# Re-planning the prologue of a two-branch mixer kernel: load order, late memsets, interleaved transposes, and w3 work between the last kv tiles

## The chip, the cores and the metric

One core of one Trainium2 chip. The metric is the device time of one execution in microseconds. "Span" is the time that the profile covers, about 2 us less than the device time. Engines: PE (TensorE), ACT (ScalarE), DVE (VectorE), POOL (GpSimd), SP (its queue issues most DMAs).

## The reference, cut to what matters

```python
x = A_x; xn = layernorm(x)                       # 2048 x 448
# branch A, linear attention, 16 heads of 28
q, k, v = split(xn @ wqkv)
phi(t) = concat(softmax(t @ w_phi), softmax(-(t @ w_phi)))
kv = phi(k)^T v ; z = sum(phi(k))
A = (phi(q) kv / (phi(q) z + 1e-6)) @ wo
# branch B
h  = gelu(layernorm(xn) @ w1); hs = shift(h) @ w2; x1 = xn + hs
B  = x1 + gelu(layernorm(x1) @ w3) @ w4
out = x + A + B
```

## The kernel before

A recorder notes each operation with the 32-byte granules of each half of the partitions that it reads and writes, keeps program order on each engine, and puts semaphore waits where granules overlap. So where a memset stands in the program decides what waits for it. All elementwise operations show as one helper line (L198), activations as L194, matmuls as L186, transposes on PE as L190, plain DMAs as L204.

The parts that the change touches (cuts marked `# ...`):

```python
GRAIN = 32
# ... hT is 4 chunks of S+8 columns, bf16; gelu writes hT[:, m, 2 + 512*g : ...]
R.dma(wphi ..., "ACT")
load_x(0, 2); load_x(2, 2)
load_rows(wqk, A_wqkv[:, 0:896])             # q and k weights, rows of 1792 bytes
load_rows(w1, B_w1)
load_x(4, 4); load_x(8, 4)
load_rows(wv, A_wqkv[:, 896:1344]); load_x(12, 4)
# ... on POOL, ahead of everything else:
R.ew(pool, "memset", xn[:, :, D:512], 0.0)
# ... masks
R.ew(pool, "memset", hT[:, :, 0:2], 0.0)
R.ew(pool, "memset", hT[:, :, S + 2:S + 4], 0.0)
# ... g_tok, vaug, kvq pads

ln1_stats(0, 2); ln1_stats(2, 2); ln1_apply(0, 2, [dve]); ln1_apply(2, 2, [dve])
for t in (1, 0):
    for pair in range(2):
        weight_T(t, pair)                    # transposes wq, wk: 8 on PE, 1 copy on ACT
phi_blocks()
for i in range(4):
    xn_T(i)                                  # 4 transposes on PE into bank 0 or 1, 1 copy on ACT
ln1_stats(4, 4); ln1_stats(8, 4); ln1_apply(4, 4, [pool, dve])
for g in range(NG):
    for m in range(NM):
        w1_chunk(g, m)                       # 4 matmuls, gelu on ACT
        if g < 2:
            fold(1 - g, m)                   # 4 small matmuls, copy on ACT
    # ... stats and apply of later tiles
    for i in range(4 * g + 4, min(4 * g + 8, NT)):
        xn_T(i)
    if g < 2:
        for i in range(4 * g, 4 * g + 4):
            v_tile(i)
for i in range(NT + 2):                      # the k phase
    if i < NT:
        k_tile(i)
    if i >= 2:
        kv_tile(i - 2)
    # ... v_tile or w2_tile, q_chunk
kv_copy()
rot[0] = (3, 4, 7)                           # accumulation banks of w2 and final tiles
# ... four groups of 14 w3 chunks, with num, w2 and final tiles between them;
# num_tile uses banks 5 and 6
```

A tile is 128 tokens, a chunk 112 or 128 columns of a weight for the 512 tokens of a group; there are four groups. `xn_T` transposes a tile of xn, and its copy out of PSUM is xnT. `fold` multiplies a part of wk or wq with w_phi, so `k_tile` and `q_chunk` give phi(k) and phi(q) at once. `kv_tile` adds one tile's phi(k)^T v, `kv_copy` and `kv_blocks` bring the sum into the form (kvq) that `num_tile` needs for the numerator and denominator of A, and the final tiles are the last two products and the sum. A bank is one of the kernel's eight PSUM buffers.

The softmax here doesn't subtract the row's maximum and nothing guards it: scores larger than these inputs give would overflow.

## Time and profile before

| | before |
|---|---|
| device time | 219.07 us median of 4 runs (218.12 to 219.85) |
| the profiled run | 217.17 us, span 215.1 us |
| PE busy | 194.1 us, 90% of the span |
| k phase starts | 46.58 us |
| first num tile starts | 98.55 us |

The page's busy line of PE, then PE's busy tenths and the granted clock in 40 slices of 5.4 us:

```profile
PE 194.1 (90%) x1161; PEld 108.2 (50%) x1161; DVE 115.5 (54%) x259; ACT 94.9 (44%) x168; POOL 93.2 (43%) x125
...
PE   0469798798999998959999999999999999999994
...
PEclk9997999999999999999999999999999999999999
```

PE is the bottleneck, its idle time is mostly in the first ten slices and at the 18th, and the clock dips once, in the fourth slice. The page prints full clock until the trace's first clock record, which is at 12.24 us in this trace. PE was at half clock before it: the 32 transposes that start at 8.37 us take 3.96 us, 0.12 us each, and the eight that start at 12.58 take 0.62, 0.08 each.

The timeline (start, duration, engine, line, operation, output and inputs, count; in brackets the idle time just before and what ended it; names are those of buffers, some of them shared: `hi<-in_A_wqkv` is wqk, `w` stands for w1, w2 or w3):

```profile
3.85 0.26 POOL L198 MEMSET hT<- 128x8 bf16 x2
...
8.37 3.96 PE L190 MATMUL bank<-ident,hi 128*112 128x128 bf16 x32 [8.37 <-DMA hi<-in_A_wqkv_dram]
...
15.72 1.28 ACT L194 ACT_TABLE_LOAD   x1
...
17.75 0.60 ACT L194 ACTIVATE hT<-bank 112x512 bf16<-112x512 f32 x1 [0.74 <-PE bank L186]
...
27.07 1.03 PE L186 MATMUL bank<-xnT,w 128*112 128x512 bf16 x4
...
32.98 0.80 PE L190 MATMUL bank<-ident,xn 128*128 128x128 bf16 x8 [1.05 <-ACT xnT L194]
...
41.53 0.80 PE L190 MATMUL bank<-ident,xn 128*128 128x128 bf16 x8 [0.82 <-ACT xnT L194]
43.08 3.66 PE L186 MATMUL bank<-xnT,w 128*112 128x512 bf16 x16 [0.76 <-ACT xnT L194]
46.58 0.92 PE L186 MATMUL bank<-wpk,xnT 128*128 128x448 bf16 x4
...
94.59 0.56 PE L186 MATMUL bank<-phik,vaug 128*128 128x224 bf16 x4 [2.18 <-POOL phik L198]
...
98.55 0.62 PE L186 MATMUL bank<-kvq,eq_lo 112*128 112x128 bf16 x8 [0.36 <-DVE kvq L198]
```

To be seen: hT's pads are cleared at 3.85 us and nobody ever waits for them; the second group's first w1 chunk starts at 27.07; three waits for xnT copies (two banks, four tiles in a row) stand between 32 and 43 us; the k phase starts at 46.58; the last kv tile waits 2.2 us for POOL.

The stretches (start:end, length, busy time and count of PE, PEld, DVE, ACT and POOL, granted clock, DMA share, GB/s), the first of which is where the clock dips:

```profile
15.60:19.00 3.40, 3.24 (x11) 1.87 (x12) 3.23 (x10) 2.42 (x4) 1.42 (x3) 0.51 1.04 340
...
92.00:98.50 6.50, 4.00 (x29) 2.11 (x26) 4.30 (x8) 3.84 (x6) 5.40 (x8) 1.00 0.02 5
```

### The profile page before, as it was taken

Reading aid. Unit: us, or ns where it says so; the run is one execution under the profiler, and the core shown is the slowest. Engines: PE = TensorE matmul, PEld = TensorE weight load, DVE = VectorE, ACT = ScalarE, POOL = GpSimd, SP = SyncE. Lnnn points to the kernel's source line nnn. Section 1 sums busy time; section 2 is a strip of 40 time slices with the busy share of each in tenths; the row PEclk is TensorE's granted clock in tenths of the full one; section 3 lists DMA queues with packets and bytes.
Section 4 is the critical chain, followed back from the end, with each engine's and each line's share of the span. In section 5 each row is a group of like instructions: output and inputs, shape, how many; then the busy total and the mean of one; then the engine's idle time right before and its main releaser. Section 6 shows DMA issues by size and latency. Waiting matters only on the chain.

```text
span 215.1 us, 3027 instructions
## 1 busy us (share of the span) xinstructions
PE 194.1 (90%) x1161; PEld 108.2 (50%) x1161; DVE 115.5 (54%) x259; ACT 94.9 (44%) x168; POOL 93.2 (43%) x125
## 2 busy tenths in 40 slices
PE   0469798798999998959999999999999999999994
PEld 0345465454666555635555545545555555555552
DVE  6479624007788886867995654733552435414121
ACT  2197574869566666754443312332342234222000
POOL 7806800004566897575228333039213331235310
PEclk9997999999999999999999999999999999999999
DMA  5999900000000013002231312302531111102101
GB/s 180 318 301 301 285 13 0 0 5 0 0 0 3 0 35 63 0 3 49 57 68 24 70 47 52 70 21 49 72 71 44 33 42 46 46 21 52 43 21 43
DMA packets 26987, 13.70 MB, mean 64 GB/s; under 512 B 18398, under 2 KB 26526, under 8 KB 26974
## 3 DMA queue, kind: packets, MB, share of 16 engines
q1 hardware_dynamic: 26512, 13.49, 24.9%
q8 instruction: 9, 0.15, 0.3%
q10 hardware_dynamic: 462, 0.03, 0.2%
q14 instruction: 4, 0.03, 0.0%
HBM read 7.48 MB, written 1.84 MB: 43 GB/s over the span
## 4 chain that ended last, share of the span: by engine, by line
PE 77%; DVE 7%; ACT 5%; POOL 5%; DMA 3%; issue 1%; SPq 0%
PE bank L186 74%; POOL phik L198 3%; DMA hi<-in_A_wqkv_dram 3%; DVE st L198 3%; PE bank L190 3%; DVE ksum L198 2%; POOL g_tok L198 1%; ACT phik L194 1%; DVE mv L198 1%; ACT hi L194 1%; ACT xnT L194 1%; ACT hT L194 1%; ACT L194 1%; DVE kvq L198 1%; DVE rks L198 1%
## 5 line engine op out<-in xcount | busy, mean ns | idle before, releaser
L194 ACT ACTIVATE phik<-bank 128x512 bf16<-128x512 f32 (+1 forms) x88 | 49.2, 581 | 68.0 <-PE bank L186 68.0
L198 DVE TENSOR_TENSOR vaug<-bank,vaug 128x464 f32<-128x464 f32 (+2 forms) x64 | 33.3, 520 | 43.0 <-PE bank L186 27.6
L186 PE MATMUL bank<-gT,w 128*128 128x512 bf16 x224 | 53.9, 379 | 0.0
L186 PE MATMUL bank<-w,phik 128*128 128x448 bf16 x224 | 45.0, 352 | 0.0
L198 POOL TENSOR_TENSOR phik<-phik,rks 128x896 bf16<-128x896 bf16 x16 | 27.1, 1698 | 35.8 <-DVE rks L198 35.6
L198 POOL TENSOR_TENSOR xnT<-vaug 128x448 bf16<-128x448 f32 x16 | 15.1, 942 | 59.1 <-DVE vaug L198 59.1
L186 PEld LDWEIGHTS bank<-w,phik 128*128 128x128 bf16 x224 | 21.9, 98 | 20.9
L186 PEld LDWEIGHTS bank<-gT,w 128*128 128x128 bf16 x224 | 21.2, 98 | 21.6
L198 DVE TENSOR_REDUCE ksum<-phik 128x32 f32<-128x896 bf16 x16 | 17.3, 1083 | 19.0 <-ACT phik L194 19.0
L194 ACT ACTIVATE hi<-bank 112x512 bf16<-112x512 f32 (+1 forms) x20 | 12.4, 681 | 14.4 <-PE bank L186 7.4
L198 POOL TENSOR_TENSOR vaug<-xn,xtok 128x448 f32<-128x448 bf16 x16 | 16.5, 1031 | 5.3 <-DVE vaug L198 5.3
L186 PE MATMUL bank<-xnT,w 128*112 128x512 bf16 x64 | 17.0, 407 | 1.4 <-ACT xnT L194 1.4
L186 PE MATMUL bank<-xnT,wpq 128*112 128x512 bf16 x64 | 16.4, 379 | 0.0
L186 PE MATMUL bank<-w,hT 112*128 112x448 bf16 x64 | 14.8, 353 | 0.0
L186 PE MATMUL bank<-wo,xnT 128*128 128x448 bf16 x64 | 14.7, 352 | 0.0
L186 PE MATMUL bank<-wpk,xnT 128*128 128x448 bf16 x64 | 14.7, 352 | 0.0
L194 ACT ACTIVATE hT<-bank 112x512 bf16<-112x512 f32 x16 | 9.6, 598 | 10.9 <-PE bank L186 10.8
L198 DVE CAST vaug<-bank 128x448 bf16<-128x448 f32 x16 | 9.5, 593 | 8.6 <-PE bank L186 7.8
L186 PE MATMUL bank<-wv,xnT 128*128 128x448 bf16 x64 | 13.7, 352 | 0.0
L186 PE MATMUL bank<-phik,vaug 128*128 128x224 bf16 x64 | 8.8, 259 | 3.7 <-POOL phik L198 3.7
L198 DVE RECIPROCAL vaug<-bank 128x16 f32<-128x16 f32 x16 | 4.0, 250 | 14.2 <-PE bank L186 14.2
L190 PE MATMUL bank<-ident,hi 128*112 128x128 bf16 x32 | 3.8, 312 | 8.5 <-DMA hi<-in_A_wqkv_dram 8.4
(63 smaller groups left out, 204.6 us busy)
## 6 DMA issues: line engine op xcount, KB each, us to landing
out_dram<-vaug SPq DMA_DIRECT2D x16, 112.0 KB, 1.7
w<-in_B_w_dram SPq DMA_DIRECT2D x1, 1568.0 KB, 15.1
xtok<-in_A_x_dram SPq DMA_DIRECT2D x3, 448.0 KB, 7.4
w<-in_B_w_dram SPq DMA_DIRECT2D x1, 1344.0 KB, 11.7
hi<-in_A_wqkv_dram SPq DMA_DIRECT2D x1, 672.0 KB, 6.4
xtok<-in_A_x_dram SPq DMA_DIRECT2D x2, 224.0 KB, 3.1
w<-in_B_w_dram SPq DMA_DIRECT2D x1, 392.0 KB, 8.5
w<-in_B_w_dram SPq DMA_DIRECT2D x1, 336.0 KB, 6.9
```

The lines of the kernel that those rows point to most:

```text
L186: self.op("PE", lambda e: e.matmul(out, lhsT, rhs, start=start, stop=stop, skip_group_check=True), [out], [lhsT, rhs])
L190: self.op("PE", lambda e: e.transpose(out, in_, ident), [out], [in_, ident])
L194: self.op("ACT", lambda e: e.activation(out, in_, func, **kw), [out], [in_] + aps)
L198: self.op(eng, lambda e: getattr(e, name)(out, *args, **kw), [out], aps)
```

## The change

The intent: let PE start earlier (wk first and alone, on a second queue; only its 16 transposes ahead of the first group; memsets that are not needed yet moved behind the norms), keep it from waiting for xnT copies (transposes put between v tiles and w1 chunks), and cover the waits at the end of the k phase with w3 chunks.

```diff
-        R.dma(wphi ..., "ACT")
-        load_x(0, 2)
+        load_x(0, 2)
+        R.dma(wphi ..., "ACT")
+        load_c(wqk[:, :, D:2 * D], A_wqkv[:, D:2 * D], "ACT")
         load_x(2, 2)
-        load_rows(wqk, A_wqkv[:, 0:896])
         load_rows(w1, B_w1)
+        load_rows(wqk[:, :, 0:D], A_wqkv[:, 0:D])
         load_x(4, 4)
+        load_rows(wv, A_wqkv[:, 896:1344])
         load_x(8, 4)
-        load_rows(wv, A_wqkv[:, 896:1344])
# ... POOL: only ident, mhalf, xn[:, 0:4] pads, rsel and masks stay in front; the rest becomes
+        def late_1(): ...   # xn[:, 4:NT] pads
+        def late_2(): ...   # half of vaug's pads, then both hT pads
+        def late_3(): ...   # the other half of vaug, g_tok, kvq
-        for t in (1, 0):
-            for pair in range(2):
-                weight_T(t, pair)
         phi_blocks()
+        weight_T(1, 0); weight_T(1, 1)
         for i in range(4):
             xn_T(i)
+        late_1()
         ln1_stats(4, 4)
+        ln1_apply(4, 4, [pool, dve])
+        late_2()
+        for m in range(NM):
+            w1_chunk(0, m); fold(1, m)
+            if m % 2 == 1:
+                weight_T(0, m // 2)
+        ln1_stats(8, 4)
+        v_tile(0); xn_T(4); xn_T(5); v_tile(1); xn_T(6); v_tile(2); xn_T(7); v_tile(3)
# ... groups 1 to 3 in the same manner; for group 2: w1, two xn_T, w1, two xn_T, w1, w1
# the k phase: the last two kv tiles and kv_copy leave the loop
-        rot[0] = (3, 4, 7)
+        rot[0] = (3, 4)                      # num_tile takes its two banks from 5, 7, 6
+            if g == 0: steps = [             # one entry after each w3 chunk
+                    [kv_tile(14)], [kv_tile(15), kv_copy], [], [kv_blocks],
+                    [g_apply(4..7)], [num_tile(0)], [w2_tile(8), g_T(4), g_T(5)], [num_tile(1)],
+                    [w2_tile(9), g_T(6), g_T(7), o_T(0)], [num_tile(2)], [w2_tile(10), o_T(1)],
+                    [num_tile(3)], [w2_tile(11), ln_scale(8..11)], [o_T(2)]]
```

No matmul is added or removed. The built program shows one thing that the diff does not say: ACT's load of the gelu table now waits for POOL.

```
ACT, before:  5 L194 LoadActFuncSet
              6 L194 Activation hT<-bank 112x512 [waits s_PE]
ACT, after:   7 L194 LoadActFuncSet [waits s_POOL]
              8 L194 Activation hT<-bank 112x512 [waits s_PE]
```

More of the change, by code (lines that the diff above doesn't have):

```diff
@@ L330, in load_rows, with load_c @@
             R.dma(dst[0:64, 3, :], src[384:448, :])
+        def load_c(dst, src, eng):
+            R.dma(dst[:, 0:3, :], src[0:384, :].rearrange("(c p) d -> p c d", p=128), eng)
+            R.dma(dst[0:64, 3, :], src[384:448, :], eng)
+        load_x(0, 2)
         R.dma(wphi[0:DH, :].rearrange("e (h f) -> e h f", h=H), A_w_phi.rearrange("h e f -> e h f"), "ACT")
-        load_x(0, 2)
+        load_c(wqk[:, :, D:2 * D], A_wqkv[:, D:2 * D], "ACT")
         load_x(2, 2)
-        load_rows(wqk, A_wqkv[:, 0:896])
         load_rows(w1, B_w1)
+        load_rows(wqk[:, :, 0:D], A_wqkv[:, 0:D])
         load_x(4, 4)
+        load_rows(wv, A_wqkv[:, 896:1344])
         load_x(8, 4)
-        load_rows(wv, A_wqkv[:, 896:1344])
         load_x(12, 4)
@@ L344, in bass_parallel_sum__linear_kernel_hedgehog__mixer_s_mlp__prompt_kernel @@
         R.dma(w4[:, :, :], B_w4.rearrange("(c p) d -> p c d", p=128))
+        mb = maskb[0:CR, :].rearrange("p (h e) -> p h e", h=4)
+        rv = rsel[0:DH, :].rearrange("p (h e) -> p h e", h=4)
+        vp = vaug.rearrange("p t (h e) -> p (t h) e", e=HP)
+        kq = kvq[0:CR, :, :].rearrange("p b (h e) -> p b h e", e=HP)
         R.ew(dve, "memset", wqk[64:128, 3, :], 0.0)
@@ L354, in bass_parallel_sum__linear_kernel_hedgehog__mixer_s_mlp__prompt_kernel @@
              [ident], [ident])
-        R.ew(pool, "memset", xn[:, :, D:512], 0.0)
         R.ew(pool, "memset", mhalf[:, :], -0.5)
+        R.ew(pool, "memset", xn[:, 0:4, D:512], 0.0)
+        R.ew(pool, "memset", rsel[0:DH, :], 0.0)
+        R.op(pool, lambda e: e.affine_select(rv, rv, pattern=[[0, 4], [-1, DH]], compare_op=ALU.not_equal,
+                                             fill=1.0, base=0, channel_multiplier=1), [rsel[0:DH, :]], [rsel[0:DH, :]])
         R.ew(pool, "memset", maskb[0:CR, :], 1.0)
-        mb = maskb[0:CR, :].rearrange("p (h e) -> p h e", h=4)
         R.op(pool, lambda e: e.affine_select(mb, mb, pattern=[[-DH, 4], [0, DH]], compare_op=ALU.is_ge,
@@ L363, in bass_parallel_sum__linear_kernel_hedgehog__mixer_s_mlp__prompt_kernel, with late_1, late_2, late_3 @@
              [maskb[0:CR, :]], [maskb[0:CR, :]])
-        R.ew(pool, "memset", rsel[0:DH, :], 0.0)
-        rv = rsel[0:DH, :].rearrange("p (h e) -> p h e", h=4)
-        R.op(pool, lambda e: e.affine_select(rv, rv, pattern=[[0, 4], [-1, DH]], compare_op=ALU.not_equal,
-                                             fill=1.0, base=0, channel_multiplier=1), [rsel[0:DH, :]], [rsel[0:DH, :]])
-        R.ew(pool, "memset", hT[:, :, 0:2], 0.0)
-        R.ew(pool, "memset", hT[:, :, S + 2:S + 4], 0.0)
-        R.ew(pool, "memset", g_tok[:, :, D:512], 0.0)
-        vp = vaug.rearrange("p t (h e) -> p (t h) e", e=HP)
-        R.ew(pool, "memset", vp[:, :, DH:HP], 0.0)
-        R.ew(pool, "memset", vp[:, :, DH:DH + 1], 1.0)
-        R.ew(pool, "memset", kvq[0:CR, :, :], 0.0)
-        kq = kvq[0:CR, :, :].rearrange("p b (h e) -> p b h e", e=HP)
-        for b in range(8):
-            R.ew(pool, "tensor_copy", kq[:, b, :, DH + 1:DH + 2], mb[:, :, 0:1])
+        def late_1():
+            R.ew(pool, "memset", xn[:, 4:NT, D:512], 0.0)
+        def late_2():
+            R.ew(pool, "memset", vp[:, 0:8 * H, DH:HP], 0.0)
+            R.ew(pool, "memset", vp[:, 0:8 * H, DH:DH + 1], 1.0)
+            R.ew(pool, "memset", hT[:, :, 0:2], 0.0)
+            R.ew(pool, "memset", hT[:, :, S + 2:S + 4], 0.0)
+        def late_3():
+            R.ew(pool, "memset", vp[:, 8 * H:NT * H, DH:HP], 0.0)
+            R.ew(pool, "memset", vp[:, 8 * H:NT * H, DH:DH + 1], 1.0)
+            R.ew(pool, "memset", g_tok[:, :, D:512], 0.0)
+            R.ew(pool, "memset", kvq[0:CR, :, :], 0.0)
+            for b in range(8):
+                R.ew(pool, "tensor_copy", kq[:, b, :, DH + 1:DH + 2], mb[:, :, 0:1])
         def ln_stats(stt, mvt, src, i):
@@ L508, in num_tile @@
             r = i % 2
-            bs = [banks[5], banks[6]]
+            bs = [bank(5, 7, 6), bank(5, 7, 6)]
             for s in range(2):
@@ L557, in bass_parallel_sum__linear_kernel_hedgehog__mixer_s_mlp__prompt_kernel @@
         ln1_apply(2, 2, [dve])
-        for t in (1, 0):
-            for pair in range(2):
-                weight_T(t, pair)
         phi_blocks()
+        weight_T(1, 0)
+        weight_T(1, 1)
+        rot[0] = (5, 6, 7)
         for i in range(4):
             xn_T(i)
+        late_1()
         ln1_stats(4, 4)
-        ln1_stats(8, 4)
-        ln1_apply(4, 4, [pool, dve])
-        rot[0] = (5, 6, 7)
-        for g in range(NG):
-            for m in range(NM):
-                w1_chunk(g, m)
-                if g < 2:
-                    fold(1 - g, m)
-            if g == 0:
-                ln1_stats(12, 4)
-                ln1_apply(8, 4, [pool, dve])
-            if g == 1:
-                ln1_apply(12, 4, [pool, dve])
-            for i in range(4 * g + 4, min(4 * g + 8, NT)):
-                xn_T(i)
-            if g < 2:
-                for i in range(4 * g, 4 * g + 4):
-                    v_tile(i)
+        ln1_apply(4, 4, [pool, dve])
@@ new lines, in bass_parallel_sum__linear_kernel_hedgehog__mixer_s_mlp__prompt_kernel @@
+        late_2()
+        for m in range(NM):
+            w1_chunk(0, m)
+            fold(1, m)
+            if m % 2 == 1:
+                weight_T(0, m // 2)
+        ln1_stats(8, 4)
+        v_tile(0)
+        xn_T(4)
+        xn_T(5)
+        v_tile(1)
+        xn_T(6)
+        v_tile(2)
+        xn_T(7)
+        v_tile(3)
+        ln1_apply(8, 4, [pool, dve])
+        for m in range(NM):
+            w1_chunk(1, m)
+            fold(0, m)
+        ln1_stats(12, 4)
+        v_tile(4)
+        xn_T(8)
@@ L583, in bass_parallel_sum__linear_kernel_hedgehog__mixer_s_mlp__prompt_kernel @@
+        xn_T(9)
+        v_tile(5)
+        xn_T(10)
+        v_tile(6)
+        xn_T(11)
+        v_tile(7)
+        ln1_apply(12, 4, [pool, dve])
+        late_3()
+        w1_chunk(2, 0)
+        xn_T(12)
+        xn_T(13)
+        w1_chunk(2, 1)
+        xn_T(14)
+        xn_T(15)
+        w1_chunk(2, 2)
+        w1_chunk(2, 3)
+        for m in range(NM):
+            w1_chunk(3, m)
         rot[0] = (0, 1, 2, 3, 4, 5)
-        for i in range(NT + 2):
-            if i < NT:
-                k_tile(i)
+        for i in range(NT):
+            k_tile(i)
@@ L587, in bass_parallel_sum__linear_kernel_hedgehog__mixer_s_mlp__prompt_kernel @@
             if i >= 2:
                 kv_tile(i - 2)
-            if i < NT:
-                if i % 2 == 0:
-                    v_tile(8 + i // 2)
-                else:
-                    w2_tile(i // 2)
-                    if i % 8 == 7:
-                        ln_scale(mv2, rs2, i // 2 - 3, 4)
-                q_chunk(*divmod(i, 4))
-                if i == 9:
-                    for j in range(4):
-                        g_apply(j)
-                if i >= 12:
-                    g_T(i - 12)
@@ L602, in bass_parallel_sum__linear_kernel_hedgehog__mixer_s_mlp__prompt_kernel @@
-        kv_copy()
+            if i % 2 == 0:
+                v_tile(8 + i // 2)
+            else:
+                w2_tile(i // 2)
+                if i % 8 == 7:
+                    ln_scale(mv2, rs2, i // 2 - 3, 4)
+            q_chunk(*divmod(i, 4))
+            if i == 9:
+                for j in range(4):
+                    g_apply(j)
+            if i >= 12:
+                g_T(i - 12)
         R.ew(pool, "memset", o_tok[:, :, D:512], 0.0)
-        rot[0] = (3, 4, 7)
+        rot[0] = (3, 4)
@@ L608, in bass_parallel_sum__linear_kernel_hedgehog__mixer_s_mlp__prompt_kernel @@
                 fill.append(lambda g=g: [g_apply(4 * g + 4 + j) for j in range(4)])
-            if g == 0:
-                fill.append(kv_blocks)
             for j in range(4):
@@ L618, in bass_parallel_sum__linear_kernel_hedgehog__mixer_s_mlp__prompt_kernel @@
                 if g < 2:
-                    fill.append(lambda i=i + 8: w2_tile(i))
+                    if True:
+                        fill.append(lambda i=i + 8: w2_tile(i))
                     if j == 3:
                         fill.append(lambda i=4 * g + 8: ln_scale(mv2, rs2, i, 4))
-                if g + 1 < NG:
-                    fill.append(lambda i=i + 4: g_T(i))
+                if g + 1 < NG and j in (1, 2):
+                    fill.append(lambda i=4 * g + 2 * j + 2: [g_T(i), g_T(i + 1)])
                 if i > 0:
                     fill.append(lambda i=i - 1: o_T(i))
-            n = 0
+            if g == 0:
+                steps = [
+                    [lambda: kv_tile(14)], [lambda: kv_tile(15), kv_copy], [], [kv_blocks],
+                    [lambda: [g_apply(4 + j) for j in range(4)]], [lambda: num_tile(0)],
+                    [lambda: w2_tile(8), lambda: g_T(4), lambda: g_T(5)], [lambda: num_tile(1)], [lambda: w2_tile(9), lambda: g_T(6), lambda: g_T(7), lambda: o_T(0)],
+                    [lambda: num_tile(2)], [lambda: w2_tile(10), lambda: o_T(1)],
+                    [lambda: num_tile(3)], [lambda: w2_tile(11), lambda: ln_scale(mv2, rs2, 8, 4)],
+                    [lambda: o_T(2)]]
+            else:
+                steps = [fill[len(fill) * k // FC:len(fill) * (k + 1) // FC] for k in range(FC)]
             for fc in range(FC):
                 w3_chunk(g, fc)
-                while n < len(fill) * (fc + 1) // FC:
-                    fill[n]()
-                    n += 1
+                for f in steps[fc]:
+                    f()
         o_T(NT - 1)
```

## The prediction

> **What bounds it.** TensorE: the page gives PE 194.1 us of a 215.1 us span; the chain of waits is 77% PE, and one unbroken run of matmuls from 98.5 to 212.3 us. Only PE's idle time can be won: 21.0 us. By the timeline and the stretches: 8.4 us before the first transpose (waits for the q/k weights' DMA), 3.4 us more up to 24 us, 2.6 us in three waits between 31 and 44 us (xnT copies), 3.0 us inside the k phase (phik chain, not touched), 2.2 us at 92.4 (last kv tile waits for POOL's phik), 0.4 us at 98.2 (kvq), and the tail (not touched). Work is only reordered, nothing is removed.
>
> **End of the k phase.** Now w3 chunks (0.87 us each) stand between kv tiles 14 and 15 and before the kv blocks. phik of tile 15 is ready about 2.6 us after the last q chunk, covered by two w3 chunks and a kv tile (2.1 us): 2.2 shrinks to about 0.6, and 0.4 vanishes. Gain 1.9 us. I take back 0.3: in the first w3 group num tiles now come every two w3 chunks, about 2.9 us of PE for 3.6 us of DVE (2.2 for the num tile, 1.4 for w2 and its statistics).
>
> **Prologue.** wk alone (392 KB, second queue) should land near 6.5 instead of 8.2. By the Trainium skill ("DMA: Bandwidth & Descriptors", Issuing engines are not separate DMA queues) both queues share the same DMA engines; the trace's 300 GB/s is the limit already, so the second queue gains only order. Sixteen transposes instead of 32 precede the first xnT; the POOL norm scales no longer wait for memsets (8.58 before, about 5.7 after). The first w1 matmul moves from 15.8 to about 12.3.
>
> But most of this is given back by one dependency. The pad columns of hT are now cleared in "late_2", behind the second group's norms on POOL, and the first gelu writes the same 32-byte granule. The built order shows ACT's gelu table load waiting for POOL there. Path: x tiles 4-7 land 11.2 (same bytes ahead of them), statistics 2.9 (DVE), scale 1.5, two applies 1.4, vaug memsets about 1.1, hT: about 18.4. Then table load 1.28, so the first gelu is at about 19.7, against 17.75 before. PE fills its three w1 banks and stops about 17 to 20.8. By the skill ("TensorE: Matmul & The Clock Gate", Part 1) an idle window re-throttles the clock; in the trace before it was 0.66 between 15 and 20 us, so a slow stretch near 20 us is likely again. From there ACT limits (0.60 + 0.54 per w1/fold pair, 0.94 per weight transpose copy). Walking the banks by hand: second group's w1 at about 28.9 (27.1 before), but interleaved v tiles remove the xnT waits, and k starts near 45.9 instead of 46.6. Gain 0.7 us.
>
> **Sum.** 0.7 + 1.9 - 0.3 = 2.3 us: 216.6 us, 1.1% faster; range 213.9 to 218.5. Chances: faster by over 2% 0.17, within 2% 0.80, slower 0.03.
>
> **What would show it.** First PE work at 6 to 7 us; ACT's second table load preceded by a wait of several us for POOL, ending at 18 to 19; a PE gap of 3 to 4 us before 21; k phase starting 45 to 46.6; the wait before the last kv tile under 1 us; no gaps over 0.5 us after 100 us; PE busy about equal.
>
> **What would make it wrong.** x tiles 4-7 landing earlier or POOL quicker (a first gelu at 16 would give 3 us more); the clock staying low after the stall (up to 2 us lost); wk's DMA delaying x; two accumulation banks (3, 4) instead of three stalling w2 or the final tiles; DVE falling behind in the first w3 group.

## The result, and the profile after

The changed kernel took 213.18 us, median of 4 runs (213.00 to 213.39). The ratio to before is 0.973, 95% interval 0.969 to 0.977. A ratio here is the mean time of one kernel's fast runs over that of the other's of the same rounds, so not quite the ratio of the medians that I quote; the runs that are over 1.5% above the fastest of the same kernel are left out of it. Predicted were 216.6 us and a range that ended at 213.9: the gain was 5.9 us, not 2.3.

The page's busy line of PE, its busy tenths and the clock:

```profile
PE 195.7 (93%) x1161; PEld 108.5 (51%) x1161; DVE 116.4 (55%) x259; ACT 94.5 (45%) x168; POOL 93.4 (44%) x128
...
PE   1687899998999989999999999999999999999994
...
PEclk9999999999999999999999999999999999999999
```

The timeline, the lines that answer to those of before:

```profile
12.15 1.95 PE L186 MATMUL bank<-xnT,w 128*112 128x512 bf16 x4 [0.69 <-ACT xnT L194]
...
17.17 0.58 POOL L198 MEMSET hT<- 128x8 bf16 x2
...
17.20 1.31 PE L186 MATMUL bank<-xnT,w 128*112 128x512 bf16 x4
...
17.67 1.28 ACT L194 ACT_TABLE_LOAD   x1 [5.58 <-POOL hT L198]
...
18.97 0.60 ACT L194 ACTIVATE hT<-bank 112x512 bf16<-112x512 f32 x1
...
19.46 0.54 ACT L194 ACTIVATE wpk<-bank 128x448 bf16<-128x448 f32 x1
19.89 0.60 ACT L194 ACTIVATE hT<-bank 112x512 bf16<-112x512 f32 x1
...
20.05 0.37 PE L186 MATMUL bank<-bd,hi 112*128 112x112 bf16 x4 [1.54 <-ACT wpk L194]
...
27.20 1.07 PE L186 MATMUL bank<-xnT,w 128*112 128x512 bf16 x4
...
43.87 0.92 PE L186 MATMUL bank<-wpk,xnT 128*128 128x448 bf16 x4
...
91.86 0.56 PE L186 MATMUL bank<-phik,vaug 128*128 128x224 bf16 x4 [0.45 <-POOL phik L198]
...
96.16 0.61 PE L186 MATMUL bank<-kvq,eq_lo 112*128 112x128 bf16 x8
...
106.01 0.40 PE L186 MATMUL bank<-kvq,eq_lo 112*128 112x128 bf16 x4 [0.44 <-DVE vaug L198]
```

The clock line is not the whole truth here either. The first clock record of this trace is at 17.77 us, and until then PE was at half clock: the w1 chunk at 12.15 us takes 1.95 us, the one at 20.26 takes 1.03.

What they show, as differences of the two spans, 215.1 and 211.2 us:

- **Prologue.** The hT memset is where I feared it, and ACT waits 5.6 us for it. The second group's first w1 chunk starts at 27.20, against 27.07 before: the earlier start is used up entirely. Yet the k phase starts at 43.87 instead of 46.58, 2.7 us earlier; this is won after 27 us, where the three waits for xnT are gone.
- **End of the k phase.** From the start of the k phase to the first num tile it is now 52.3 us instead of 52.0, but six w3 chunks of 0.87 us lie in it instead of three: 2.6 - 0.3 = 2.3 us won.
- **w3 phase.** From the first num tile to the start of the last addition it was 113.7 us (212.28 - 98.55); three chunks fewer would make 111.1; it is 112.3 (208.44 - 96.16). So 1.15 us are lost, part of it in the 0.44 us wait for DVE shown above.
- 2.7 + 2.3 - 1.15 is 3.9 us, the difference of the spans. The medians differ by 5.9. The other 2 us are not in these two traces.

### The profile page after: what moved, and what is told of

Its sections match the earlier page's. It is cut to its first block, busy times and chain, and to the rows that moved or that the text cites. A ratio compares the mean times of both kernels' runs of the same rounds, so it can differ in the third digit from the quotient of the medians.

```text
span 211.2 us, 3034 instructions
## 1 busy us (share of the span) xinstructions
PE 195.7 (93%) x1161; PEld 108.5 (51%) x1161; DVE 116.4 (55%) x259; ACT 94.5 (45%) x168; POOL 93.4 (44%) x128
## 4 chain that ended last, share of the span: by engine, by line
PE 66%; DVE 13%; POOL 10%; ACT 6%; issue 2%; DMA 2%; POOLq 0%; DVEq 0%; ACTq 0%
PE bank L186 64%; DVE vaug L198 5%; DVE st L198 3%; POOL phik L198 3%; POOL g_tok L198 3%; POOL rs L198 2%; ACT hi L194 2%; DVE xn L198 2%; DVE ksum L198 2%; DMA xtok<-in_A_x_dram 2%; PE bank L190 1%; ACT phik L194 1%; ACT hT L194 1%; DVE mv L198 1%; POOL vaug L198 1%
## 5 line engine op out<-in xcount | busy, mean ns | idle before, releaser
L186 PE MATMUL bank<-xnT,w 128*112 128x512 bf16 x64 | 17.8, 418 | 0.7 <-ACT xnT L194 0.7
L186 PE MATMUL bank<-wv,xnT 128*128 128x448 bf16 x64 | 14.7, 353 | 0.3 <-ACT wpk L194 0.3
L198 POOL TENSOR_SCALAR rs<-mv 128x4 f32<-128x4 f32 (+1 forms) x18 | 3.7, 207 | 21.8 <-DVE mv L198 20.8
L198 POOL TENSOR_SCALAR g_tok<-xn,rs 128x448 bf16<-128x448 bf16 x16 | 11.2, 715 | 0.2
L194 ACT ACTIVATE eq_lo<-bank 112x512 bf16<-112x512 f32 x16 | 8.7, 596 | 5.8 <-PE bank L186 5.8
```

The source lines that it names most:

```text
L186: self.op("PE", lambda e: e.matmul(out, lhsT, rhs, start=start, stop=stop, skip_group_check=True), [out], [lhsT, rhs])
L194: self.op("ACT", lambda e: e.activation(out, in_, func, **kw), [out], [in_] + aps)
L198: self.op(eng, lambda e: getattr(e, name)(out, *args, **kw), [out], aps)
```

## The experiments

Each ran on a chip together with runs of the kernel before, whose median was 217.2 to 219.7 us on three chips. The changed kernel itself hardly moves (213.18 and 213.20 us). "Landing" times are those of the last of the 16 completions of a load in the trace's record, and half-clock windows are from its clock record; both count from the span's start.

### e0: the kernel before, again

No edit.

> The kernel before, unchanged, to see every run's clock and span. Theory A (the trace I predicted from was of a run about 2 us faster than the usual one: the profiled run took 217.17 us, the four timed ones 218.1 to 219.9): timed runs 218 to 220 us, and a profile whose prologue differs (more TensorE time at half clock, or late DMA landings). Theory B (profiled and timed runs differ by a fixed overhead): the new profile again near 217.2, spans of the timed runs near 215. If A holds, some of the 5.9 us is a matter of the baseline and not of my sum.

Measured: 219.55 us, median of 6 (216.55 to 219.90); the profiled run took 219.65, span 217.9. Its stretches:

```profile
15.00:21.80 6.80, 6.11 (x24) 3.26 (x23) 6.49 (x21) 4.08 (x7) 4.07 (x8) 0.50 1.06 286
21.80:96.90 75.10, 67.63 (x416) 40.65 (x415) 43.89 (x80) 50.91 (x98) 36.54 (x34) 1.00 0.13 32
96.90:100.30 3.40, 3.40 (x16) 1.82 (x14) 0.67 (x3) 1.19 (x2) 3.40 (x6) 0.51 0.19 40
```

Theory A holds for this pair of traces. After the first clock record the clock was at half for 6.8 us in the prologue and for 3.4 us just after the wait for the last kv tile, 10.2 us in all; in the trace that I predicted from it was 3.4 us. The k phase began at 47.94 instead of 46.58 and the stretch from there to the first num tile took 53.45 instead of 51.97: 1.36 + 1.48 = 2.8 us, the whole difference of the two spans. Same kernel, same work, no other difference.

Whether the usual run looks like this one is less clear. The record has the mean granted clock, and one 3.4 us window takes 0.008 off it. Of the 55 runs of the kernel before none reads 1.000; 44 read 0.992 (one window), nine 0.984 and two 0.976 or 0.977, like this profiled run. So a window somewhere is the rule, and three are rare. But the 44 runs with 0.992 took 216.66 to 220.69 us: the recorded clock, which leaves out what lies before its first record, does not order the times.

### e1 and e11: the new prologue with the old end

```diff
 # from the k phase on, the lines of before
-        for i in range(NT):
+        for i in range(NT + 2):
# ... and kv_copy(), rot (3, 4, 7), num_tile on banks 5 and 6
```

> The new prologue with the old end of the k phase and the old w3 phase. Theory (sum of the two traces): k phase starts at 43.9 us as in the changed kernel, 2.7 us before the old one, and the end is as before: 2.7 us faster than before by the traces, 3.5 to 4.7 if the usual run of before has a worse prologue; so 214.4 to 216.4 us. Rival (the end gives most of the measured 5.9 us): under 1.5 us faster, over 217.5 us.

> e1 again, on the same chip as e4 again. Theory (half-clock windows after the wait before the last kv tile): 214.2 to 216.5 us in two clusters, most in the upper one, median 215.5 to 216.2.

Measured: e1 216.00 us (214.24 to 216.50), ratio to before 0.988 (0.983 to 0.993); e11 on another chip 214.58 us (214.41 to 216.16), ratio 0.983 (0.979 to 0.987). In e11 five of six runs lie at 214.4 to 214.8, where I had expected most in the upper cluster. So the prologue gives about 1.2 to 1.7%, 2.7 to 3.7 us, about half of the whole or more.

### e2: the old prologue with the new end

```diff
 # up to the k phase, the lines of before; then those of the change
+        for i in range(NT):
+            bs = [bank(5, 7, 6), bank(5, 7, 6)]
```

> The old prologue with the new end of the k phase and the new w3 phase. Theory: 2.3 us won up to the first num tile less 1.1 us lost in the first w3 groups, so 1.2 us faster than before, 217.3 to 218.3 us. My prediction's term: 1.6 us faster. Rival (end gives most): over 3 us faster, under 216 us.

Measured: 217.32 us (215.25 to 219.20), ratio 0.9925 (0.986 to 0.999), so 0.7% or about 1.6 us, which is what I had predicted for this part (1.9 - 0.3). The profiled run, at 219.03, was one of the slow ones (half clock at 24 to 28 us and again at 45 to 48); I read nothing else from it.

### e3 and e14: hT's pads cleared early

```diff
         R.ew(pool, "memset", mhalf[:, :], -0.5)
+        R.ew(pool, "memset", hT[:, :, 0:2], 0.0)
+        R.ew(pool, "memset", hT[:, :, S + 2:S + 4], 0.0)
# ... and the same two lines taken out of late_2()
```

> The changed kernel with the two memsets of hT's pad columns put back ahead of the norms on POOL (0.3 us there). Theory (the late memset holds ACT's first gelu, and through it PE, and costs several us): the wait of ACT for POOL's hT (5.6 us) is gone, table load at about 12.1, first gelu near 14.0 instead of 19.0, first w1 of the second group at 23 to 25 instead of 27.2, k start at 40.5 to 42.5 instead of 43.9, total 210 to 212 us. Rival (the norms' statistics limit the prologue, so PE only waits elsewhere): the second group's w1 stays within 1 us of 27.2 and the total over 212.3 us.

> e3 again, unchanged, for comparison on the same chip: 209.4 to 210.4 us, no half-clock window after 18 us.

Measured: 210.08 us (209.42 to 210.33), e14 209.91 us (209.36 to 210.63); ratios 0.962 and 0.960. The timeline of e3:

```profile
12.36 1.28 ACT L194 ACT_TABLE_LOAD   x1
14.38 0.60 ACT L194 ACTIVATE hT<-bank 112x512 bf16<-112x512 f32 x1 [0.74 <-PE bank L186]
...
24.19 1.07 PE L186 MATMUL bank<-xnT,w 128*112 128x512 bf16 x4
...
40.85 0.92 PE L186 MATMUL bank<-wpk,xnT 128*128 128x448 bf16 x4
```

The theory holds: table load at 12.4, first gelu at 14.4 instead of 19.0, second group at 24.2 instead of 27.2, k phase at 40.85 instead of 43.87, and 3.1 us less in all. Two memsets of 0.3 us together, in the wrong place, cost the change a third of what it could have won.

### e5: the kernel before with only the transposes interleaved

```diff
-            for i in range(4 * g + 4, min(4 * g + 8, NT)):
-                xn_T(i)
             if g < 2:
-                for i in range(4 * g, 4 * g + 4):
-                    v_tile(i)
+                v_tile(t); xn_T(t + 4); xn_T(t + 5); v_tile(t + 1)
+                xn_T(t + 6); v_tile(t + 2); xn_T(t + 7); v_tile(t + 3)   # t = 4 * g
# ... and in group 2 two xn_T after each of the first two w1 chunks
```

> The kernel before with only the transposes of groups 1 to 3 put between v tiles and w1 chunks, as the change has them; loads, memsets, first group and end as before. Theory (the start of the changed kernel gains nothing net because the hT wait eats it, both traces have the second group's first w1 at 27.1 and 27.2; the whole prologue gain of 2.7 us comes from removing the three xnT waits of 1.05, 0.82 and 0.76 us): k start 2.4 to 2.9 us earlier relative to the second group's first w1, total about as e1, 1.0 to 1.4% faster than before. Rival (the early loads and norms gave it): under 0.4% faster.

Measured: 214.01 us (211.92 to 214.39), ratio 0.981 (0.976 to 0.986). This is more than I expected: 1.9% (unclear by the 2% rule), as much as or more than the whole new prologue. In its timeline of PE:

```profile
25.32 1.07 PE L186 MATMUL bank<-xnT,w 128*112 128x512 bf16 x4
...
41.78 0.92 PE L186 MATMUL bank<-wpk,xnT 128*128 128x448 bf16 x4
```

With the old loads, the old memsets and the old first group, the k phase starts at 41.78 us: 2.1 us earlier than in the changed kernel. The wait for xnT in the first group (1.04 us before) is gone too, which I had not counted. This profile has half-clock windows at 15.1 and 90.2, and its run took 214.02; the fastest took 211.92.

### e9 and e10: all of the change but its start, beside the changed kernel

```diff
 # e9: e5 up to the k phase, then the lines of the change; e10: the change, no edit
```

> e5 with the changed kernel's end: all of the change except its start (loads, memsets, norms and first group are those of before). Theory (the start as shipped costs about 2 us net: e5's k phase began at 41.8 us, the changed kernel's at 43.9; the hT wait is larger than what the early loads win): faster than the changed kernel on the same chip by 0.5 to 2.5 us, 211 to 212.7 us. Rival (the start helps or is neutral): not faster than the changed kernel, 213 us or more.

> The changed kernel, unchanged, on the same chip as the other runs of this call, for comparison: 212.9 to 213.6 us, no half-clock window after 18 us in the profile.

Measured on the same chip: e9 212.20 us (210.36 to 212.96), ratio 0.970; e10 213.20 us (213.05 to 213.37), ratio 0.976. So the start as shipped made the change slower, by 1.0 us in the medians, and the two ranges do not overlap. The size is less sure than the sign: e9's own profile fell on its slowest run, with 6.8 us at half clock from 15.2 us on, and there the k phase starts at 43.75 us, as late as in the changed kernel. Part of the expectation for e10 failed in a useful way: its profile does have a half-clock window, right after the hT wait.

```profile
16.70:20.10 3.40, 1.39 (x13) 0.76 (x12) 1.94 (x6) 2.41 (x4) 2.04 (x7) 1.00 1.06 308
20.10:23.50 3.40, 3.40 (x21) 2.46 (x22) 0.00 (x0) 3.40 (x7) 1.75 (x3) 0.50 1.09 333
```

PE was busy for only 1.39 us of the 3.4 before the window, and the next 3.4 us ran at half clock. Yet this run took 213.32 us, 0.3 us more than the run of the first profile, 213.00, which had no window after 18 us. By their clocks two of e10's six runs have such a window (0.991; 213.32 and 213.37 us) and four have none (213.05 to 213.30), so it costs about 0.2 us. In it ACT is busy without a break, and in the first profile, without the window, PE waits for ACT three times between 20 and 26 us (0.40, 0.27 and 0.19), so most of the slow clock is hidden. In e0 it was not: there one more window cost 1.36 us in the prologue and one 1.48 at the last kv tile.

### e4, e12 and e8: idle PE time filled with thrown-away work

```diff
 # e4, e12 (on e1)
             if i >= 2:
+                if i == NT + 1:
+                    for _ in range(8): R.mm(banks[2][:, :], gT[:, 0, 0, 0:128], gT[:, 0, 1, :], True, True)
                 kv_tile(i - 2)
 # e8 (on before): the same, and
+        warm(56)                             # transposes of the identity, ahead of weight_T
# ... warm(14) after xn_T(1), warm(8) after xn_T(3)
```

> e1 (new prologue, old end) with 8 matmuls of 128x512 whose result is overwritten, put into the 2.2 us wait before the last kv tile. They do no useful work. Theory (in most runs of e1 and of before that wait lets TensorE's clock fall to half for a 3.4 us window just after it, about 1.7 us lost; e1's six runs fall into 214.2 to 214.6 and 215.9 to 216.5): the upper cluster disappears, all runs 214 to 215 us, median about 1.5 us under e1's 216.0. Rival (the two clusters have another cause): still two clusters, median within 0.5 us of 216.0, or slower by the 1.7 us of added matmuls.

> e4 again, on the same chip as e1 again; the first time the two were on different chips and each was 1.2 to 1.3% faster than before. Theory: no run over 215.8 us and a median 0.8 us or more under e1's of this call. Rival (the fill changes nothing): medians within 0.5 us.

> The kernel before with idle TensorE time filled by work that is thrown away: 56 transposes of the identity ahead of the first transposes, 14 and 8 in the xnT waits of the first group, 8 matmuls before the last kv tile. No order is changed otherwise. Theory (about 2 us of before's usual time, and all of its spread of 216.6 to 220.3, is TensorE at half clock after its own idle gaps): no half-clock window after about 12 us in the profile, runs within 1 us of each other at 215 to 216.5 us, so 2 to 3.5 us faster than before with no useful reordering. Rival (the clock is a by-product and costs nothing on the path): within 1 us of before, spread as before.

Measured: e4 214.74 us (214.22 to 215.75), ratio 0.987, the same ratio as e1. e12 took 214.62 us (214.16 to 215.30) and e11, without the fill, 214.58 (214.41 to 216.16). So the fill did not lower the median; the rival's mark is met. No run of e4 or e12 was over 215.8, while five of the twelve runs of e1 and e11 were, which fits the theory. Their clocks say more: of these twelve runs of e1 and e11 the six at 0.992 took 214.79 to 216.50 us and the six at 1.000 took 214.24 to 214.66. So the two clusters are runs with and without a window. Of the twelve of e4 and e12 three read 0.992, and in the one of them that was profiled the window lies at 21.9 to 25.4 us, not after the filled wait. With the fill, then, windows were fewer (three runs of twelve against six), but in the call that had both kernels they were few even without it, and no gain in the median is shown. (The expectation of e12 speaks of different chips; the record gives chip 9 for both earlier calls.) e8 took 217.56 us (215.65 to 218.43), no faster than before (ratio 0.999). Its profile fell on its fastest run, and there the clock rose at 6.51 us, during the thrown-away transposes, and was at full speed from then on:

```profile
15.60:19.00 3.40, 3.40 (x27) 2.18 (x26) 3.26 (x11) 3.36 (x7) 1.76 (x5) 1.00 1.03 337
```

The other five runs were 1.7 to 2.8 us longer. I have no trace of them, but three at 0.992 took 217.36 to 217.57 us, two at 0.984 took 217.91 and 218.43. So in five of six runs the fill did not keep the windows away, and more windows went with longer runs. Where they fell, and why the fill did not prevent them, is not known.

### e6 and e17: the first w3 group relaxed

```diff
 # on e3, group 0
-  num_tile at steps 5, 7, 9, 11; w2_tile at 6, 8, 10, 12
+  num_tile at steps 5, 8, 11, 13; w2_tile 8 to 10 at 6, 9, 12
+  # group 1 begins with w2_tile(11); its g_apply stand behind the first final tile
```

> e3 with the first w3 group relaxed: num tiles every three w3 chunks instead of every two, w2 tile 11 moved into the second group, the second group's four norm applications on POOL put behind the first final tile. Theory (in the changed kernel PE waits there for DVE, 0.2 and 0.4 us at 102 and 106 us, and 0.3 us at 118 for a bank that waits on POOL, about 1 us in all): these waits go, 209.0 to 209.5 us against e3's 210.1, and the best of all versions. Rival (DVE lag only moves): within 0.3 us of e3.

> e6 again, on the same chip as the combined version, so that the load order alone differs: 208.6 to 209.6 us.

Measured: 209.04 us (208.44 to 209.72) and 209.17 us (208.13 to 209.44), against 210.08 and 209.91 of e3 and e14: about 0.9 us less. They were run at other times. So this rests on e3's kernel being steady. The waits of 0.44 us at 106 and 0.3 us at 118 are gone from the timeline. The 1.15 us lost in the w3 phase is thus largely DVE's and POOL's lag.

### e13: wk first, but on the same queue

```diff
 # on e3
-        load_c(wqk[:, :, D:2 * D], A_wqkv[:, D:2 * D], "ACT")
         load_x(2, 2)
+        load_c(wqk[:, :, D:2 * D], A_wqkv[:, D:2 * D], "SP")
```

> e3 (hT pads early) with wk loaded from the SP queue, after both first x loads, instead of from ACT's. Theory (as the skill says of issuing engines: the queues share the same DMA engines, so only the order counts): wk lands within 0.7 us of e3's 6.6 to 7.3, total within 0.6 us of e3 on the same chip. Rival (the second queue itself brings data sooner): over 1 us slower.

Measured: 209.36 us (206.99 to 210.49) against 209.91 (209.36 to 210.63) of e14 on the same chip; without its slow run (210.49) e13's median is 209.00. The timeline of PE of e14 (second queue), then of e13 (same queue):

```profile
5.41 0.57 PE L190 MATMUL bank<-ident,hi 128*112 128x128 bf16 x3 [0.52 <-DMA hi<-in_A_wqkv_dram]
7.33 1.60 PE L190 MATMUL bank<-ident,hi 128*112 128x128 bf16 x13 [1.36 <-DMA hi<-in_A_wqkv_dram]
...
12.45 1.95 PE L186 MATMUL bank<-xnT,w 128*112 128x512 bf16 x4 [0.69 <-ACT xnT L194]
```

```profile
6.09 2.09 PE L190 MATMUL bank<-ident,hi 128*112 128x128 bf16 x16 [1.21 <-DMA hi<-in_A_wqkv_dram]
...
11.69 1.95 PE L186 MATMUL bank<-xnT,w 128*112 128x512 bf16 x4 [0.69 <-ACT xnT L194]
```

On the second queue the large part of wk comes 0.7 us sooner, but its last 64 rows, which every chunk's fourth transpose needs, land only at 7.2 us. On one queue everything has landed at 6.5 us, and the first w1 chunk starts 0.76 us earlier. The rival (over 1 us slower) is refuted; the theory's total holds over all six runs (0.55 us less) but not without the slow one (0.9 us less). The second queue brought nothing that shows.

The load order is not all that differs between the two profiles, though. The k phase starts at 39.62 us in e13 and at 41.45 in e14, far more than 0.76 apart. The first clock record, until which PE is at half clock, is at 15.19 us in e13 and at 18.52 in e14. Over the six profiles of versions with early hT pads the start of the k phase goes with that moment and not with the queue: 15.15 and 39.89 (e17, second queue), 15.19 and 39.62 (e13, same queue), 15.69 and 40.04 (e16, same queue), 17.41 and 40.85 (e3), 17.89 and 40.91 (e6), 18.52 and 41.45 (e14, all second queue). So about half a microsecond is lost for each microsecond that the clock rises later, and the mean clocks of these runs, 0.998 to 1.000, do not show it.

### e15: the kernel before with wqk in two halves

```diff
-        load_rows(wqk, A_wqkv[:, 0:896])
+        load_rows(wqk[:, :, D:2 * D], A_wqkv[:, D:2 * D])
+        load_rows(wqk[:, :, 0:D], A_wqkv[:, 0:D])
```

> The kernel before with wqk loaded in two halves of 896-byte rows, k first, both on the SP queue; nothing else changed. With the old start, all five profiles show x tiles 4 to 7 landing at 10.9 to 11.4 us, three or more of the 16 engines 1 to 1.6 us behind the rest; with the new start 9.7 to 10.2. Theory (the wide 1792-byte rows make some engines late): x tiles 4 to 7 land at 9.6 to 10.3, first transpose at 6.5 to 7.3 instead of 8.4, total within 1% of before since PE waits later anyway. Rival (something else in the old start): landing still 10.9 to 11.4.

Measured: 216.15 us (215.62 to 217.01), ratio 0.989 (0.984 to 0.993), a little more than the 1% allowed. x tiles 4 to 7 landed at 10.44 us: between the theory's range and the rival's, against 11.2 in the first profile of before and 9.8 in that of the change. The first transpose:

```profile
6.38 3.55 PE L190 MATMUL bank<-ident,hi 128*112 128x128 bf16 x32 [6.38 <-DMA hi<-in_A_wqkv_dram]
```

It starts 2.0 us earlier than in the profile of before. It needs only the k half, which had landed at 6.48 us; but the whole of wqk had landed at 8.01 us too, instead of 8.88, with the same bytes in the same queue. About half of the late landing of x goes away with one load of wide rows cut in two; whether the width or the cut does it, and what the rest is, stays open. One profile of each is thin ground for tenths of a microsecond.

### e16: the combination

e6 with e13's load order.

> e6 (hT pads early, num tiles spread) with wk on the SP queue as in e13. Theory: the two gains are of different phases and add: e14 to e13 was 0.5 us, e3 to e6 1.0 us, so 208.2 to 208.9 us, the fastest of all. Rival: the gains overlap, 209 us or more.

Measured: 208.56 us (207.76 to 208.93), ratio 0.952; e17 on the same chip 209.17 us. The fastest version of all: 4.6 us less than the changed kernel's median, and correct. That the load order adds to the rest is not shown: the ranges of e16 (207.76 to 208.93) and e17 (208.13 to 209.44) overlap, and in their profiles the k phase starts at 40.04 and 39.89 us.

| version | median us | ratio to before |
|---|---|---|
| before (four runs of the first comparison) | 219.07 | 1 |
| e2 new end only | 217.32 | 0.993 |
| e15 before, wqk in halves | 216.15 | 0.989 |
| e1, e11 new prologue only | 216.00, 214.58 | 0.988, 0.983 |
| e5 interleaving only | 214.01 | 0.981 |
| the change, e10 | 213.18, 213.20 | 0.973, 0.976 |
| e9 the change without its start | 212.20 | 0.970 |
| e3, e14 hT pads early | 210.08, 209.91 | 0.962, 0.960 |
| e6, e17 and num tiles spread | 209.04, 209.17 | 0.961, 0.955 |
| e16 and wk on the same queue | 208.56 | 0.952 |

## Why the prediction was wrong, point by point

The step that failed is the prologue's: "most of this is given back by one dependency ... Gain 0.7 us". The dependency was there, and e3 proves its cost, but it gave back far less than the walk had it: 0.13 us at the second group's first w1 chunk instead of 1.8, and the prologue gained 2.7 us in the traces, 2.7 to 3.7 in e1 and e11. The end of the k phase with its w3 group was right (1.6 us predicted, about 1.6 measured in e2, with an interval of 0.3 to 3.0). Of the signs that the prediction names, three did not come: PE's gap before 21 us was 1.5 us (18.51 to 20.05) and not 3 to 4, the table load's wait ended at 17.67 and not at 18 to 19, and the k phase started at 43.87 and not at 45 to 46.6. The sum was too small by 3.6 us. By the traces three terms were mis-sized, and one was missing.

1. **The baseline (missing, about 1.9 us).** "2.3 us: 216.6 us" subtracts what one trace showed from the median of other runs. That trace was of a 217.17 us run; the median was 219.07. The difference between two profiles of the same kernel (e0) is half-clock time: 3.4 us in one and 10.2 in the other, and the extra time sits exactly in those windows. The changed kernel's runs lie within 0.4 us of each other (213.00 to 213.39), those of before within 1.7 in the same comparison and from 216.7 to 220.7 over the later ones. I had named a slow stretch as a risk to the new kernel only. What the record shows of the other runs: every later run of before has at least one recorded window, eight of the changed kernel's ten have none. What it does not show: why runs of before with the same recorded clock differ by up to 4 us, and the four runs of the first comparison have no clock on record. So the 1.9 us is a measured difference between trace and median, half-clock time explains it in one pair of traces, and for the usual run its cause stays open. Nor does the change lessen half-clock time as a whole. From PE's first work (4.28 us) to its first clock record (17.77) the changed kernel runs 13.5 us at half clock, the kernel before 3.9 (8.37 to 12.24) and its window of 3.4. Here most of that is hidden behind the hT wait; with the hT pads early it is not (e13).

2. **The prologue (0.7 predicted, 2.7 measured).** "The first gelu is at about 19.7" was 18.97, because I let x tiles 4 to 7 land at 11.2 with "same bytes ahead of them"; they landed at 9.8, and statistics began at 10.08. (Nor was the trace's 300 GB/s "the limit already": between 14.35 and 17.77 us the changed kernel's loads moved 387.) "ACT limits (0.60 + 0.54 per w1/fold pair, 0.94 per weight transpose copy)" adds durations. The timeline shows the starts of consecutive activations 0.49 and 0.43 us apart: 0.11 us less each, 1.1 us for the ten of the first group. The Trainium skill says so ("ScalarE: Activation LUTs", What ACT_TABLE_LOAD costs, the paragraph on the ACTIVATE instruction: "Back-to-back ACTIVATEs overlap by ≈ 93 ns"); the trace has 110 ns. I did not look it up. Together, about 1.8 us, these are the 1.7 us between "second group's w1 at about 28.9" and 27.20. From there to the k phase I allowed 17.0 us and it took 16.7.

3. **The end of the k phase (1.9 predicted, 2.3 measured).** The wait before the last kv tile was 0.45 us where I had put 0.6; the rest is rounding of the same kind.

4. **The w3 phase (0.3 lost predicted, 1.15 measured).** "About 2.9 us of PE for 3.6 us of DVE" was the right mechanism. The lag of four num tiles, and two accumulation banks behind a POOL busy with four norm applications, make it three waits instead of one. e6 took about 0.9 us back.

5. **What the hand walk did not show.** I credited the prologue's gain to an earlier start that was partly given back. e5 and e9 show that the start as shipped was given back in full: interleaving alone starts the k phase at 41.78 us in e5's profile and at 43.75 in e9's, which has one half-clock window more, the change at 43.87. By the medians of e9 and e10 it was given back with 1.0 us more. The early loads and norms are worth something only with the hT pads early (40.85).

The clock window at "near 20 us" did come, in e10's profile and not in the first one. It cost about 0.2 us.

## What to carry to other kernels

When memsets are moved behind other work, look in the built program for who now waits for them: a pad that shares a granule with real output makes the whole output wait, and here 0.3 us of memset cost 3.1 us. Interleave the steps that an in-order engine would otherwise do in a row against two buffers; here that alone gave 1.9%. Before subtracting a gain from a median, check that the trace was of a median run, and where a bottleneck engine's clock depends on its own idle time, count the removed idle gap and also the slow window that may follow it. And look at matmul durations, not at the page's clock, before the first clock record: an early start in short pieces left PE at half clock until 15.2 to 18.5 us in the versions with early hT pads. I tried no fill there, so what a warm clock at 12 us would be worth is open.

## What the Trainium skill lacked or had wrong

- "TensorE: Matmul & The Clock Gate", Part 1, gives the half clock, the free-running window of about 3.4 us and the need to avoid idle gaps of that length. Windows of 3.4 us and multiples agree with the traces here. But a wait of 2.2 us was enough: PE was busy for 1.24 of the 3.41 us before the half-clock window at 96.9 to 100.3 us (e0). Windows made two runs of one kernel differ by 2.5 us, 1.1% (217.17 and 219.65).
- The same page gives no busy share for the clock to rise. Counted in steps of 3.41 us from the clock records, PE was busy for 0.97 of the step before the first rise in the kernel before; in the changed kernel the steps from 4.11 us on had 0.49, 0.74, 0.80 and 1.00, and the clock rose after the last. Over the 19 traces, by the modelled ends of the matmuls, every rise followed a step of 0.84 or more and none a step of 0.80 or less. For the fall no such share comes out: steps of 0.36 to 0.59 preceded the falls, and others of 0.43 to 0.60 preceded none.
- The same page: no word on where a half-clock window costs nothing. Directly after the hT wait it cost about 0.2 us, since ACT was the limit (e10, runs with and without it).
- "DMA: Bandwidth & Descriptors", Issuing engines are not separate DMA queues, says that DMAs started from different engines run on the same 16 DMA engines, and the runs agree: the second queue gave nothing (209.91 with it, 209.36 without). It has no figure for what this costs a small load on the second queue: the last 64 rows of wk landed at 7.20 us instead of 6.50 (e14, e13).
- The same page (Rules for kernel authors) advises large transfers for bandwidth. Loading wqk as two loads with 896-byte rows instead of one with 1792-byte rows let all of it land at 8.01 instead of 8.88 us, its first half at 6.48, and x tiles 4 to 7 at 10.4 instead of 11.2 (e15, one profile of each); I found no page that tells of this.
- No page says that a profile's granted clock reads 1.00 before its first clock record: the first w1 chunk of e13 at 11.69 us took 1.95 us for four matmuls, against about 1.03 later, with a clock of 9 tenths or more in every slice.
